# Two PSUM pools throughout instead of a late single ring, and W1-W2 moved behind a cast on GpSimd

## The chip, the cores and the metric

The kernel runs on one core of one Trainium2 chip. The metric is the device time of one execution in microseconds (us). It is compared as a median over several executions. A profiled execution gives, beside its own time, the span from the first to the last instruction and a row for every instruction of each engine: PE (TensorE, with its weight loads as PEld), DVE (VectorE), ACT (ScalarE), POOL (GpSimd) and SP (the queue that issues nearly all DMAs).

## The reference

A cross attention between 512 tokens `x` and 32 state rows in each of 8 batches x 8 heads (64 elements per head) is followed by a feed-forward layer with two input matrices.

```python
scores = scale * x @ state.T;   a  = softmax(scores);   xread = a  @ state
scores2 = scale * state @ x.T;  a2 = softmax(scores2);  sread = a2 @ x
y = concatenate([xread, sread], axis=2)      # per batch 544 tokens of 512 elements
h1 = y @ w1; h2 = y @ w2                     # 512 -> 1024
out = maximum(h1, h2) @ w_out                # 1024 -> 512
```

The maximum is rewritten as `max(h1, h2) = relu(y @ (w1 - w2)) + y @ w2`, so that the layer is `relu(y @ (W1-W2)) @ w_out + y @ (W2 w_out)`. The kernel calls `[W1-W2 | W2 w_out]` Wc: 1024 + 512 columns, three chunks of 512. For the 512 tokens of a batch, `y` is `a @ state`, so the product of the states with Wc (512 rows against 1536 columns, `SW[b]`) is made once per batch, and `a` is multiplied with that.

## The kernel before

All is written out by hand in the order in which it is issued; no scheduler changes it. Each engine runs its own instructions in that order, and so does SP with its DMAs.

**Setup.** SP first loads states and x of batch 0, W2 and W_out in pieces, W1 in two pieces, x of batch 1, the remaining states, x of batch 2. The weights are cast to bf16 on DVE and ACT (`w_cast`), W_out on POOL (`wo_cast`), W2 is transposed and multiplied with W_out (`w_wo`), which gives the third chunk of `wcat`. The first two chunks, W1-W2, are made by POOL in four pieces of 256 columns (`w_sub(0)` to `w_sub(3)`, line 389).

**A batch** goes through these steps. The x tile is cast into `xp` by POOL (`cast_x`, line 72) and once more into the compact `xc` by ACT (`compact_x`), which a DMA transposes into `xt` (`d_xt`). `u_exp` (lines 221, 224) makes the scores of two groups of heads on PE and their exponentials on ACT. `u_norm` makes sums and reciprocals on DVE (lines 228, 230) and multiplies them in on DVE or POOL (`a`, line 231). `u_sr` reads the states' side (line 244), its normalised result `sr` is transposed in `u_srt` (line 268) and copied into `sread_t` by ACT. `a` is transposed by DMA (`d_at`), in batches 0 and 1 by PE (`u_at`, line 262) and copied into `aT` by DVE. `u_sw` makes the chunks of `SW[b]` on PE (line 283, `sw_mm`), with two PSUM banks each, which DVE and ACT copy out into `swt`. `l1` (lines 311, 299, 301) makes eight tiles of relu, alternating between ACT and DVE, and `l2` adds up four output chunks (`l2_open` line 322, `l2_add` line 326, `l2_close`), each in one bank.

**Two terms.** While `wcat` isn't there, `sw_mm` multiplies the states with w1 and the negated states with w2: 16 matmuls in place of 8 for a chunk. Before, this is so for batch 0 and for chunk 1 of batch 1; chunk 0 of batch 1 uses `wcat`.

**PSUM.** There are eight banks. In the setup and for batch 0, four belong to the pool `ps` and four to the pool `acc`, which holds the sums of `w_wo` and of the output chunks. Ahead of the loop over batches 1 to 7, `one_ring` closes both and opens one pool of eight banks, used for everything in turn.

**Around the change** the order is written out so: the steps of batch 0, with `w_sub(0)` and `w_sub(1)` issued on POOL ahead of `l1(0)`; then the second cast of w1, `compact_x(1)`, `d_xt(1)`, `cast_x(1)`, `w_sub(2)`, `w_sub(3)`, the cast of the remaining states (`cast_states("P", rest)`), `load_x(3)`, the DMA transposes of the states (`d_states`, tile `sT`); then the scores of batch 1, its softmax (first half multiplied on DVE, second on POOL) and its `u_sw`, mixed with the closing of batch 0. In the loop, `fillers(b)` puts the steps of batch b+1 between the output chunks of batch b.

Of the kernel before, what the change touches and what calls it, by code (L numbers as in the profile page):

```python
# [15 lines left out]
def kernel(  # L16
# [24 lines left out]
    TWO = 2  # L41
# [6 lines left out]
    keep = ctx.enter_context(tc.tile_pool(name="keep", bufs=2))  # L48
    big = ctx.enter_context(tc.tile_pool(name="big", bufs=2))

    early = ctx.enter_context(ExitStack())
    pools = dict(ps=early.enter_context(tc.tile_pool(name="ps", bufs=4, space=bass.MemoryType.PSUM)),
                 acc=early.enter_context(tc.tile_pool(name="acc", bufs=4, space=bass.MemoryType.PSUM)))
    ctx.enter_context(tc.manual_schedule())

    def bank(dtype=F32, kind="ps"):
        return pools[kind].tile([128, 512 if dtype == F32 else 1024], dtype, tag="b", name=kind)

    def acc():
        return bank(kind="acc")  # L60

    def one_ring():
        early.close()
        pools["ps"] = pools["acc"] = ctx.enter_context(tc.tile_pool(name="ring", bufs=8, space=bass.MemoryType.PSUM))

    def copy(eng, o, i):
        if eng == "A":
            nc.scalar.copy(o, i)  # L68
        elif eng == "V":
            nc.vector.tensor_copy(o, i)  # L70
        else:
            nc.gpsimd.tensor_copy(o, i)  # L72
# [68 lines left out]
    def cast_states(eng, bs):  # L141
        qs = slice(2 * bs.start, 2 * bs.stop)
        copy(eng, s_bf[:, qs], s_f[:, qs].unsqueeze(2).to_broadcast([128, qs.stop - qs.start, 2, D]))
# [36 lines left out]
    def cast_x(b, parts=(("P", slice(0, 8)),)):  # L180
        new_x(b)
        xp = st[b]["xp"] = xio.tile([128, H, NC, 66], BF16, tag="xp", name="xp")
        nc.gpsimd.memset(xp[:, :, :, 64:65], 1.0)
        for e, hs in parts:
            copy(e, xp[:, hs, :, 0:64], xf_t[b][:, hs].rearrange("p h (c d) -> p h c d", c=NC))
# [87 lines left out]
    swt = consts.tile([128, 2, 2, WC], BF16)  # L273

    def sw_mm(b, ch, engs="VA"):
        pg = [bank(), bank()]
        two = b < TWO and ch < 2 and (b, ch) != (1, 0)
        terms = ((sbd, w1b), (sneg, w2b)) if two else ((sbd, wcat),)
        for k, (sv, w) in enumerate(terms):
            for i in range(4):  # L280
                for g in range(2):
                    gs = slice(64 * g, 64 * g + 64)
                    nc.tensor.matmul(pg[g][32 * i:32 * i + 32, :],  # L283
                                     sneg[gs, b, i, :] if k else sbd[gs, b, 2 * i + g, g, :],
                                     w[gs, i, ch * 512:(ch + 1) * 512],
                                     start=(k == 0), stop=(k == len(terms) - 1))
        return lambda: [copy(engs[g], SW[b][:, g, ch * 512:(ch + 1) * 512], pg[g]) for g in range(2)]

    def u_sw(b, *chs):
        for out_of in [sw_mm(b, ch) for ch in chs]:  # L290
            out_of()
# [43 lines left out]
    def l2_out(b):  # L335
        nc.sync.dma_start(out=out[b * L:b * L + S].rearrange("(p c) n -> p c n", c=NC), in_=OB[b][0])
# [50 lines left out]
    def w_sub(q):  # L387
        cs = slice(q * 256, (q + 1) * 256)
        nc.gpsimd.tensor_sub(wcat[:, :, cs], w1f[:, :, cs], w2f[:, :, cs])  # L389

    def w_cast(o, w, ch, engs="VA"):
        cs = slice(ch * 512, (ch + 1) * 512)
        for k in range(2):
            copy(engs[k], o[:, 2 * k:2 * k + 2, cs], w[:, 2 * k:2 * k + 2, cs])
# [77 lines left out]
    for i in range(4):  # L472
        w_wo(2, i)
    w_cast(w1b, w1f, 0)
    w_sub(0)
    w_sub(1)
    for i in range(4):
        w_wo(3, i)
    u_sw(0, 0)
# [6 lines left out]
    compact_x(1, 1)  # L486
    d_xt(1)
    cast_x(1)
    w_sub(2)
    w_sub(3)  # L490
    cast_states("P", rest)
    load_x(3)
    sT = d_states(rest)
# [23 lines left out]
    u_sw(1, 2)  # L517
    u_srt(1)
    l2_out(0)
    one_ring()  # L520
    for b in range(1, B):
        fill = fillers(b)
        if b + 2 < B:
# [39 lines left out]
```

The softmax here doesn't subtract the row's maximum and nothing guards it: scores larger than these inputs give would overflow.

## Time and profile before

| | |
|---|---|
| time, median of 4 runs | 154.5 us (153.93 to 155.42) |
| the profiled execution's own time | 154.03 us |
| its span | 152.1 us, 3012 instructions |
| PE busy | 140.2 us, 92% of the span |
| DVE, ACT, POOL busy | 83.7, 75.3, 43.6 us |
| mean granted TensorE clock | 0.989 |
| HBM read, written | 15.20 MB, 8.91 MB |

Busy time is the time in which an engine had an instruction; its share is a mean over the whole span. The chain that ended last is followed back from the last instruction, at each step to what released it, and shows what set the time at each place. In a timeline each row has start, duration, engine, line, operation, output and inputs, and in brackets how long the engine had been idle before it and what ended that.

### The profile page before, as it was taken

What the parts mean: (1) busy time and instruction counts of PE and PEld (TensorE: products, weight loads), DVE (VectorE), ACT (ScalarE), POOL (GpSimd) and SP (SyncE); (2) the same over time, 40 slices, a digit from 0 to 9 for tenths busy, and PEclk for the clock granted to TensorE, in tenths of its full rate; (3) what the DMA queues carried; (4) which work ended last, traced back from release to release, by engine and by line L of the source; (5) the groups of instructions that cost most, each with busy time, mean ns of one, the idle gap of its engine ahead of it and who ended that gap; (6) DMA issues with size and microseconds to landing.
All of it is one profiled execution on the core that took longest, in us unless ns stands there. A gap on an engine that the chain in (4) does not pass through costs nothing.

```text
span 152.1 us, 3012 instructions
## 1 busy us (share of the span) xinstructions
PE 140.2 (92%) x1236; PEld 68.1 (45%) x1255; DVE 83.7 (55%) x151; ACT 75.3 (50%) x126; POOL 43.6 (29%) x44
## 2 busy tenths in 40 slices
PE   6769999998889999999999999889999999999990
PEld 1357543333445444444454454335434534664460
DVE  5368658527965487545576554645566546631120
ACT  3056259925864656546394636553656226621010
POOL 3025219993830820190046007200500050000000
PEclk9977999999999999999999999999999999999999
DMA  4999999998999498829966992990099022602423
GB/s 92 348 397 387 387 383 328 290 154 253 113 237 286 169 192 299 266 59 209 287 214 114 264 285 101 109 378 0 2 144 343 0 34 41 274 0 67 140 101 113
DMA packets 37934, 29.89 MB, mean 196 GB/s; under 512 B 24864, under 2 KB 33312, under 8 KB 37024
## 3 DMA queue, kind: packets, MB, share of 16 engines
q1 hardware_dynamic: 37776, 29.56, 70.5%
q8 instruction: 10, 0.16, 0.4%
q10 hardware_dynamic: 144, 0.13, 0.3%
q14 instruction: 4, 0.03, 0.1%
HBM read 15.20 MB, written 8.91 MB: 159 GB/s over the span
## 4 chain that ended last, share of the span: by engine, by line
PE 61%; DMA 19%; SPq 8%; ACT 3%; DVE 2%; issue 2%; POOL 2%; ACTq 0%; POOLq 0%
PE acc L326 25%; PE ps L311 16%; DMA xf<-in_x_dram 10%; PE acc L322 6%; DMA aT<-a 6%; SPq L102 4%; SPq L105 3%; DMA xt<-xc 3%; PE ps L370 2%; PE acc L380 2%; PE ps L221 2%; PE ps L283 2%; POOL a L231 2%; PE acc L360 1%; ACT xc L68 1%
## 5 line engine op out<-in xcount | busy, mean ns | idle before, releaser
L326 PE MATMUL acc<-wo,r 128*128 128x512 bf16 x244 | 58.1, 379 | 0.3 <-issue 0.2
L326 PEld LDWEIGHTS <-r 128*128 128x128 bf16 x248 | 23.9, 98 | 28.8 <-issue 0.6
L301 DVE TENSOR_SCALAR r<-ps 128x512 bf16<-128x512 f32 x32 | 22.1, 692 | 17.8 <-PE ps L311 17.7
L231 POOL TENSOR_TENSOR a<-e,er 128x512 bf16<-128x512 bf16 x13 | 13.4, 1050 | 63.0 <-ACT e L224 31.0
L311 PE MATMUL ps<-aT,swt 128*128 128x512 bf16 x122 | 28.8, 379 | 2.5 <-DMA aT<-a 1.3
L70 DVE COPY ob<-acc 128x512 f32<-128x512 f32 (+1 forms) x17 | 11.4, 672 | 27.3 <-PE acc L326 25.5
L299 ACT ACTIVATE r<-ps 128x512 bf16<-128x512 f32 x32 | 19.2, 600 | 9.7 <-PE ps L311 9.2
L311 PEld LDWEIGHTS <-swt 128*128 128x128 bf16 x128 | 12.0, 98 | 16.9 <-issue 1.9
L68 ACT CAST swt<-ps 128x512 bf16<-128x512 f32 x24 | 12.9, 592 | 12.5 <-PE ps L283 12.4
L322 PE MATMUL acc<-swt,aT 128*128 128x512 bf16 x56 | 16.7, 380 | 1.0 <-issue 1.0
L68 ACT COPY ob<-acc 128x512 f32<-128x512 f32 (+1 forms) x16 | 9.2, 576 | 15.9 <-PE acc L326 10.9
L70 DVE CAST swt<-ps 128x512 bf16<-128x512 f32 x24 | 15.3, 682 | 1.8 <-PE ps L283 1.7
L224 ACT ACTIVATE e<-ps 128x512 bf16<-128x512 f32 x16 | 8.8, 595 | 14.7 <-PE ps L221 14.7
L72 POOL CAST xp<-xf 128x2048 bf16<-128x2048 f32 (+1 forms) x8 | 14.1, 1765 | 6.4 <-DMA xf<-in_x_dram 6.4
L68 ACT CAST xc<-xf 128x1024 bf16<-128x1024 f32 x14 | 13.9, 1050 | 0.2 <-DMA xf<-in_x_dram 0.2
L228 DVE TENSOR_REDUCE es<-e 128x16 f32<-128x512 bf16 x16 | 10.6, 662 | 2.3 <-ACT e L224 2.3
L389 POOL TENSOR_TENSOR wcat<-w1f,w2f 128x1024 bf16<-128x1024 f32 x4 | 9.8, 2476 | 3.1 <-DMA w1f<-in_moe_w_dram 3.1
L136 PE MATMUL ps<-warm 128*128 128x512 bf16 x14 | 6.1, 579 | 1.5 <-POOL warm L122 1.3
L322 PEld LDWEIGHTS <-aT 128*128 128x128 bf16 x62 | 4.7, 98 | 5.9 <-issue 2.6
L415 PE MATMUL acc<-wo,w2t 128*128 128x512 bf16 x31 | 7.2, 379 | 0.1
L283 PE MATMUL ps<-wcat,sbd 64*32 64x512 bf16 x168 | 6.7, 380 | 0.1
L221 PE MATMUL ps<-sbd,xt 128*128 128x64 bf16 x128 | 5.6, 199 | 1.1 <-DMA xt<-xc 0.6
(68 smaller groups left out, 103.8 us busy)
## 6 DMA issues: line engine op xcount, KB each, us to landing
xf<-in_x_dram SPq DMA_DIRECT2D x8, 1024.0 KB, 8.8
out_dram<-ob SPq DMA_DIRECT2D x7, 1024.0 KB, 5.0
w2f<-in_moe_w_dram SPq DMA_DIRECT2D x2, 1024.0 KB, 10.5
wof<-in_moe_w_out_dram SPq DMA_DIRECT2D x4, 512.0 KB, 11.3
w1f<-in_moe_w_dram SPq DMA_DIRECT2D x2, 1024.0 KB, 14.8
out_dram<-ob SPq DMA_DIRECT2D x3, 256.0 KB, 2.8
out_dram<-obs SPq DMA_DIRECT2D x8, 64.0 KB, 1.7
s_f<-in_state_dram SPq DMA_DIRECT2D x1, 320.0 KB, 13.7
```

Source lines behind the costliest of these rows:

```text
L68: nc.scalar.copy(o, i)
L70: nc.vector.tensor_copy(o, i)
L72: nc.gpsimd.tensor_copy(o, i)
L228: nc.vector.tensor_reduce(d["es"][:, g], d["e"][:, g].rearrange("p i c n -> p (i c) n"), axis=mybir.AxisListType.X, op=ALU.add)
L231: mul.tensor_mul(d["a"][:, g].rearrange("p c i n -> p i c n"), d["e"][:, g], d["er"][:, g].rearrange("p (i c) -> p i c", i=4).unsqueeze(3) ...
L283: nc.tensor.matmul(pg[g][32 * i:32 * i + 32, :], sneg[gs, b, i, :] if k else sbd[gs, b, 2 * i + g, g, :], w[gs, i, ch * 512:(ch + 1) * 512 ...
L299: nc.scalar.activation(out=o, in_=p, func=ACTF.Relu)
L301: nc.vector.tensor_scalar(o, p, scalar1=0.0, scalar2=None, op0=ALU.max)
L311: nc.tensor.matmul(p, SW[b][:, g, f * 128:(f + 1) * 128], AT[b][:, g, :], start=(g == 0), stop=(g == 1))
L322: nc.tensor.matmul(OB[b][1 + c], AT[b][:, g, c * 128:(c + 1) * 128], SW[b][:, g, FF:WC], start=(g == 0), stop=False)
L326: nc.tensor.matmul(OB[b][1 + c], R[b][:, f, c * 128:(c + 1) * 128], wo[:, f, :], start=False, stop=(f == NF - 1))
L389: nc.gpsimd.tensor_sub(wcat[:, :, cs], w1f[:, :, cs], w2f[:, :, cs])
```

## The change

The pools `ps` and `acc` stay as they are for the whole kernel: `one_ring` and its call are gone. So that `u_sw` still finds its six banks at once, the two banks of the third Wc chunk come from `acc` for batches from 2 on. Chunk 0 of batch 1 is made in two terms as chunk 1 is, which adds eight matmuls. `w_sub(0)` and `w_sub(1)` are issued behind `cast_x(1)`, together with the other two. On SP, DVE and ACT the order of instructions stays the same; only the bank that some copies read has another name.

```diff
-    early = ctx.enter_context(ExitStack())
-    pools = dict(ps=early.enter_context(tc.tile_pool(name="ps", bufs=4, space=bass.MemoryType.PSUM)),
-                 acc=early.enter_context(tc.tile_pool(name="acc", bufs=4, space=bass.MemoryType.PSUM)))
+    pools = {k: ctx.enter_context(tc.tile_pool(name=k, bufs=4, space=bass.MemoryType.PSUM)) for k in ("ps", "acc")}
...
-    def one_ring():
-        early.close()
-        pools["ps"] = pools["acc"] = ctx.enter_context(tc.tile_pool(name="ring", bufs=8, space=bass.MemoryType.PSUM))
...
     def sw_mm(b, ch, engs="VA"):
-        pg = [bank(), bank()]
-        two = b < TWO and ch < 2 and (b, ch) != (1, 0)
+
+        pg = [bank(kind="acc" if ch == 2 and b > 1 else "ps") for g in range(2)]
+        two = b < TWO and ch < 2
...
     w_cast(w1b, w1f, 0)
-    w_sub(0)
-    w_sub(1)
     for i in range(4):
         w_wo(3, i)
...
     cast_x(1)
-    w_sub(2)
-    w_sub(3)
+    for q in range(4):
+        w_sub(q)
     cast_states("P", rest)
...
     l2_out(0)
-    one_ring()
     for b in range(1, B):
```

## The prediction

> **What bounds the kernel now.** I read the totals first, then the chain that ended last in order of time, then the timelines of POOL, DVE and PE around the places that the diff touches, and last the groups of single lines for durations.
>
> ```profile
> PE 140.2 (92%) x1236; PEld 68.1 (45%) x1255; DVE 83.7 (55%) x151; ACT 75.3 (50%) x126; POOL 43.6 (29%) x44
> PE 61%; DMA 19%; SPq 8%; ACT 3%; DVE 2%; issue 2%; POOL 2%; ACTq 0%; POOLq 0%
> ```
>
> TensorE sets the pace and POOL looks idle. That is an average. From 42 us on, the chain is matmuls of one batch after the other, 13.96 us each (l1 starts at 42.35, then at 56.31). Before that it is a chain of hand-overs, and the change lies there:
>
> ```profile
> 12.81 15.01 DMA xf<-in_x_dram
> ...
> 27.84 1.99 ACT xc L68 x2
> 29.83 0.03 ACT swt L68
> 29.86 4.80 DMA xt<-xc
> ...
> 36.78 0.69 DVE a L231
> ...
> 39.55 0.61 PE ps L262 x8
> ...
> 42.13 0.18 ACT sread_t L68
> 42.31 0.04 issue
> 42.35 3.62 PE ps L311 x16
> ```
>
> x(1) lands at 27.82, is compacted, transposed, and goes through the scores of batch 1 to the eight transposes of `u_at(1)` (L262) at 39.55 and to `l1(1)` (L311) at 42.35. PE's own row there reads "[0.83 <-ACT sread_t L68]": it was free 0.83 us before. POOL in that stretch:
>
> ```profile
> 22.14 5.16 POOL L389 TENSOR_TENSOR wcat<-w1f,w2f 128x1024 bf16<-128x1024 f32 x2 [3.05 <-DMA w1f<-in_moe_w_dram]
> 27.25 0.24 POOL L183 MEMSET xp<- 128x32 bf16 x1
> 27.87 1.91 POOL L72 CAST xp<-xf 128x2048 bf16<-128x2048 f32 x1 [0.38 <-DMA xf<-in_x_dram]
> 29.75 4.67 POOL L389 TENSOR_TENSOR wcat<-w1f,w2f 128x1024 bf16<-128x1024 f32 x2
> 34.34 1.26 POOL L72 CAST s_bf<-s_f 128x1280 bf16<-128x1280 f32 x1
> 38.50 1.05 POOL L231 TENSOR_TENSOR a<-e,er 128x512 bf16<-128x512 bf16 x1 [2.90 <-PE ps L244]
> ```
>
> The reader is to see three things: two subtractions fill the wait for x(1); POOL has 2.90 us to spare before its half of a(1); and that half ends at 39.55, the very time at which PE starts `u_at(1)`.
>
> **The subtractions move.** In the new order POOL waits for x(1) with nothing to do, casts it at 27.87 to 29.78, and then has all four subtractions ahead. Rows follow each other at 2.30 us here (29.75, 32.05, 34.34), so the third starts at 34.34, the fourth at 36.64, the cast of the remaining states at 38.94 and ends at 40.20, and a(1)'s second half can run 40.23 to 41.28. That is 1.73 us after 39.55, with nothing else disturbed. PE has no other work to put there: it is in order, and behind `u_at(1)` stand the last adds of batch 0, `u_sw(1,2)`, the transpose of sr and `l1(1)`. From the transposes on, the way to `l1(1)` is: 0.22 (the second four; the first four need DVE's half alone) + 0.96 (39.99 to 40.95) + 0.34 (40.95 to 41.29) + 0.06 = 1.58 us. Then its second tile needs the bank that ACT empties after ob and swt (41.05 to 42.13 before, 1.08 us), which holds it about 0.4 us. So `l1(1)` runs as if it had begun at T + 1.98, with T the start of the second four transposes: 41.3 + 1.98 = 43.3, or +0.95 us against 42.35.
>
> **What it meets on DVE.** The third and fourth subtraction now run while DVE does the softmax of batch 1. They meet one DVE instruction that reads two SBUF tensors as the subtraction does: the product a (L231), at 36.78, 0.14 us after the fourth has started. The trace of before doesn't show this pair, but it shows neighbours:
>
> ```profile
> L389 POOL TENSOR_TENSOR wcat<-w1f,w2f x4: 2346/2353/2853, 22.1 to 32.1; 128x1024 bf16<-128x1024 f32 x4
> L70 DVE CAST w1b<-w1f x2: 694/774/853, 22.1 to 27.2; 128x1024 bf16<-128x1024 f32 x2
> L231 DVE TENSOR_TENSOR a<-e,er x3: 691/693/744, 12.9 to 36.8; 128x512 bf16<-128x512 bf16 x3
> ```
>
> The 2853 ns subtraction is the first, at 22.14, which began while DVE's cast of w1b ran (22.09 to 22.78): it lost 0.50 us of an overlap of 0.64. The 853 ns cast began at 27.18 inside a subtraction that ended at 27.31, and a POOL memset followed until 27.49: it lost 0.16. The 744 ns product began at 12.88 inside a POOL cast that ended at 13.08: it lost 0.05 of 0.20. Each late comer ends as if it had waited for the other, less 0.14.
>
> Lower bound: a loses 0.05, as its own row did; then +0.95 stands. Upper bound: the 853 ns cast outlasted the memset behind the subtraction too, so a may wait out the states' cast as well, until 40.20. Value taken, by the 2853 ns row (longest overlap): a waits until the fourth subtraction ends, 36.64 + 2.36 = 39.00, and takes 0.55 more. It ends at 39.55, not 37.47. Everything behind it on DVE moves by that: es and er (which POOL's half of a needs), ob of chunk 0, two swt, rr, sr, ob of chunk 2, and the copy aT, without which `l1(1)` can't begin. DVE had no gap from 37.39 to the end of aT at 41.69:
>
> ```profile
> 41.01 0.68 DVE L70 COPY aT<-ps 128x1024 bf16<-128x1024 bf16 x1
> ```
>
> So aT ends near 43.85 and `l1(1)` starts at 43.9: **+1.55 us**. POOL's side agrees: the states' cast, now behind a, ends at 40.75, a(1) at 41.8, T = 41.85, and T + 1.98 = 43.83. With the upper bound aT ends at 45.0 and the shift is +2.7.
>
> [...]
>
> **The pools.** The single ring goes, and with it the wait at 42.35, which ended with ACT's sread_t at 42.29. In the new kernel the first tile of `l1(1)` takes the bank that aT empties (41.69 before), so 0.6 us of the 0.83 would be free. It is already counted: 43.9 holds no such wait, with it the start would be some 0.6 later. With four banks the fifth tile of l1 needs the first relu. In a later batch ACT does ob, sread_t and that relu from 56.46 to 57.70, and the fifth tile starts 4 x 0.43 after 56.31, at 58.04: 0.34 us to spare. `l1(0)` already ran on four banks, 8 matmuls in 1.89 us (32.22), as fast as 16 in 3.62. Cost 0. If that cover went, ACT being late by one more copy (0.59), it is 0.25 us a batch. The third Wc chunk in the adding banks takes those of chunks 3 and 0, emptied microseconds before; its copies on ACT and DVE keep their order. Cost 0.
>
> **Eight more matmuls** in `u_sw(1,0)`: by the two forms of L283, a two-term chunk holds PE 0.56 us (37.44 to 38.00), a wcat chunk 0.35 (36.13 to 36.48), so 0.2 us. PE now waits for T anyway, which hides it; without that wait it is 0.2 on the path. Its wait for POOL's wcat goes, which had been met.
>
> **SP's queue.** The transposes of the states (issued at 35.63) wait for the states' cast, so until 40.2 to 40.75. Queued behind them on SP: xt(2) (40.67), the output of batch 0 (43.77), x(4) (44.38). With 2.22 us for the states' issue, xt(2) is issued at 43.0 and lands 4.3 to 5.3 later, by 48.3; `u_exp(2)` needs it at 47.97 + 1.55 = 49.5. x(4) is 2 us later, and its cast is not due before POOL's next product, 8 us on. The DMA engines then are busy to about 53.2 rather than 51.2, and the next aT transfer (52.23, now 53.8) comes just after. If it were caught, its landing would go from 3.3 to the 5.1 us that one of the six took, less 0.8 spare: 1.0 us. I count 0 and keep it for the range. In the stretch from 22 to 27 DVE's casts become free of POOL (0.16 us); x(1)'s landing hides that.
>
> **Sum.** Span 152.1 + 1.55 = 153.65; with the 1.9 us around the span, 154.03 becomes 155.6. The profiled run is 0.47 below the median of the four, 154.5, so against the median the forecast is **156.1 us** (+1.0%).
>
> **Rivals.** (1) POOL and DVE hardly hinder each other: +0.95, 155.5 us. For it: the 0.05 us of the 744 ns row; against: 0.50 lost at 22.14. (2) POOL goes from instruction to instruction without letting DVE in, a waits until 40.20: +2.7, 157.2 us. For it: the 853 ns cast; against: at 8 us POOL's cast of xp (0.865 us) got in between two DVE casts. (3) The other side: POOL's second half of a is there before it decides. If T falls below 42.35 - 1.98 = 40.37, the freed ring wait shows and `l1(1)` starts up to 0.6 earlier: 153.9. It needs POOL 0.95 us quicker than its rows say over six instructions; nothing speaks for that but that spans on POOL are rough. (4) Four banks are too few in every batch: 6 x 0.25 on top, 157.6 us; against it the 0.34 us to spare.
>
> **How the numbers follow.** Forecast 0.45, rival 1 0.17, rival 2 0.27, rival 3 0.05, rival 4 0.06. The four runs spread by 1.5 us, so each case has some 0.5 us to both sides. The range 154.7 to 157.8 leaves out most of rival 3 and the tails. About 1% (1.5 us) is what a measurement of this kernel can tell from no change, so 156.05 parts same from slower, through the middle of the forecast: slower 0.56 (half the forecast, nearly all of 2 and 4), same 0.41 (the other half, rival 1, rival 3), faster 0.03.
>
> **What would show it.** Right: POOL's cast of xp(1) near 27.9, four L389 rows (in the new file their number differs) back to back, the states' cast ending at 40.2 to 40.8, DVE's product a near 2.8 us long or late in its end, L311's first row near 43.9 and no idle time put down to sread_t; batches 13.96 us apart. Rival 1: a stays at 0.7 us and L311 starts at 43.3. Rival 2: a ends after 40.5 and L311 starts near 45. Rival 4: idle time on L311 put down to ACT or DVE in every batch. It is wrong altogether if L311 starts before 42.4.

## The result, and the profile after

| | before | changed |
|---|---|---|
| time, median over all executions | 155.04 us (152.17 to 158.15, 16) | 154.63 us (153.67 to 155.32, 11) |
| ratio changed / before | | 1.0103, 95% interval 1.0053 to 1.0152 |
| profiled execution: time, span | 154.03, 152.1 us | 154.06, 152.2 us |
| its `l1(1)` starts | 42.35 us | 44.01 us |
| its `l1(1)` to `l1(7)` | 85.37 us | 83.76 us |

The ratio compares, of each kernel, only executions near its fastest. So there are two results: by the ratio the change costs 1.0%, about 1.6 us, while the medians over all executions come out nearly equal. The experiments below show why: in both traced executions of before some batches wait for a transpose that comes late, and in the changed kernel's trace none does. The two profiled executions have the same time, and that is where the trace must be read most carefully: a loss of 1.66 us and a gain of 1.61 us meet in it. Line numbers of the changed kernel are five or six lower: its L225, L306 and L384 are L231, L311 and L389 of the kernel before.

The totals and the chain's shares of the changed kernel, and the clock row, each digit 3.8 us:

```profile
PE 139.8 (92%) x1244; PEld 69.1 (45%) x1263; DVE 87.2 (57%) x151; ACT 75.3 (49%) x126; POOL 44.0 (29%) x44
PEclk9955999999999999999999999999999999999999
PE 82%; DVE 8%; DMA 4%; issue 2%; ACT 1%; SPq 0%
```

DVE has 3.5 us more busy time with the same 151 instructions, and 8% of the chain instead of 2%. The timelines of POOL and DVE (start, duration, engine) show which instructions grew:

```profile
27.61 1.89 POOL L66 CAST xp<-xf 128x2048 bf16<-128x2048 f32 x1 [8.72 <-DMA xf<-in_x_dram]
29.46 9.73 POOL L384 TENSOR_TENSOR wcat<-w1f,w2f 128x1024 bf16<-128x1024 f32 x4
39.14 1.71 POOL L66 CAST s_bf<-s_f 128x1280 bf16<-128x1280 f32 x1
40.82 1.04 POOL L225 TENSOR_TENSOR a<-e,er 128x512 bf16<-128x512 bf16 x1
```

```profile
27.82 2.23 DVE L64 CAST w1b<-w1f 128x1024 bf16<-128x1024 f32 x1
37.06 2.69 DVE L225 TENSOR_TENSOR a<-e,er 128x512 bf16<-128x512 bf16 x1
43.28 0.68 DVE L64 COPY aT<-ps 128x1024 bf16<-128x1024 bf16 x1
```

POOL waits 8.72 us for x(1), casts it, and makes all four pieces of W1-W2 until 29.46 + 9.73 = 39.19. DVE's product a starts at 37.06 inside the fourth, takes 2.69 us instead of 0.69, and ends at 39.75. What stands behind it is the stretch of the chain that ended last:

```profile
37.06 2.69 DVE a L225
39.74 0.61 DVE es L222
40.35 0.02 issue
40.37 0.25 DVE er L224
40.62 0.55 DVE ob L64
41.17 1.19 DVE swt L64 x2
42.36 0.09 DVE rr L242
42.45 0.02 issue
42.47 0.29 DVE sr L243
42.76 0.60 DVE ob L64
43.36 0.61 DVE aT L64
43.97 0.04 issue
44.01 3.62 PE ps L306 x16
```

DVE runs from a to aT without a gap, and `l1(1)` begins when aT is there. The rows of `l1` in PE's timeline, first changed, then before, tell the rest:

```profile
44.01 3.62 PE L306 MATMUL ps<-aT,swt 128*128 128x512 bf16 x16 [0.23 <-DVE aT L64]
57.97 3.62 PE L306 MATMUL ps<-aT,swt 128*128 128x512 bf16 x15
```

```profile
84.23 3.62 PE L311 MATMUL ps<-aT,swt 128*128 128x512 bf16 x15
99.47 3.61 PE L311 MATMUL ps<-aT,swt 128*128 128x512 bf16 x15 [1.11 <-DMA aT<-a]
113.76 3.61 PE L311 MATMUL ps<-aT,swt 128*128 128x512 bf16 x15 [0.17 <-DMA aT<-a]
```

In the changed kernel every later batch takes 13.96 us. In before's execution the fifth `l1` came after 15.24 and the sixth after 14.29 us, both after a wait for the DMA transpose aT: 1.28 + 0.33 = 1.61 us that the changed kernel doesn't have. 1.66 - 1.61 is the whole difference. That loss was in before's profile all along; the prediction saw a landing of aT in "the 5.1 us that one of the six took" and asked only whether the change would cause one more.

### The profile page after: what moved, and what is told of

Same layout as the page of the kernel before. It is cut to its first block, busy times and chain, and to the rows that moved or that the text cites. A ratio compares the mean times of both kernels' runs of the same rounds, so it can differ in the third digit from the quotient of the medians.

```text
span 152.2 us, 3021 instructions
## 1 busy us (share of the span) xinstructions
PE 139.8 (92%) x1244; PEld 69.1 (45%) x1263; DVE 87.2 (57%) x151; ACT 75.3 (49%) x126; POOL 44.0 (29%) x44
## 4 chain that ended last, share of the span: by engine, by line
PE 82%; DVE 8%; DMA 4%; issue 2%; ACT 1%; SPq 0%
PE acc L321 32%; PE ps L306 18%; PE acc L317 8%; PE acc L410 5%; DMA xf<-in_x_dram 4%; PE ps L278 3%; PE ps L215 3%; PE ps L365 2%; PE acc L375 2%; PE ps L238 2%; DVE a L225 2%; PE ps L399 2%; PE acc L355 1%; DVE w1b L64 1%; PE ps L197 1%
## 5 line engine op out<-in xcount | busy, mean ns | idle before, releaser
L225 POOL TENSOR_TENSOR a<-e,er 128x512 bf16<-128x512 bf16 x13 | 13.4, 1049 | 58.6 <-ACT e L218 30.0
L306 PE MATMUL ps<-aT,swt 128*128 128x512 bf16 x122 | 28.8, 379 | 0.8 <-DVE aT L64 0.2
L306 PEld LDWEIGHTS <-swt 128*128 128x128 bf16 x128 | 12.2, 98 | 14.8 <-DVE swt L64 0.5
L62 ACT CAST swt<-ps 128x512 bf16<-128x512 f32 x18 | 10.0, 588 | 13.8 <-PE ps L278 13.7
L64 DVE CAST swt<-ps 128x512 bf16<-128x512 f32 x18 | 11.6, 681 | 0.7 <-PE ps L278 0.7
L384 POOL TENSOR_TENSOR wcat<-w1f,w2f 128x1024 bf16<-128x1024 f32 x4 | 9.7, 2458 | 0.0
L130 PE MATMUL ps<-warm 128*128 128x512 bf16 x14 | 5.3, 510 | 1.6 <-POOL warm L116 1.3
L215 PEld LDWEIGHTS <-xt 128*128 128x128 bf16 x128 | 5.1, 101 | 2.6 <-ACT xt L62 0.7
```

The source lines that it names most:

```text
L215: nc.tensor.matmul(p[:, k * 64:k * 64 + 64], d["xt"][:, 4 * i + 2 * g + cp, :], sbd[:, b, 2 * i + g].rearrange("p u n -> p (u n)"), start= ...
L225: mul.tensor_mul(d["a"][:, g].rearrange("p c i n -> p i c n"), d["e"][:, g], d["er"][:, g].rearrange("p (i c) -> p i c", i=4).unsqueeze(3) ...
L306: nc.tensor.matmul(p, SW[b][:, g, f * 128:(f + 1) * 128], AT[b][:, g, :], start=(g == 0), stop=(g == 1))
```

## The experiments

The question was first whether DVE's product a really waits for the subtraction, then why the late transposes come and go. Theory A: moving the subtractions costs 1.5 to 2 us at `l1(1)`, pools and two terms nothing. Rivals: the four banks cost something in every batch (B); later, the place of DMAs on SP's queue decides the late transposes (C), or the length of PE's instruction stream does (D).

**The pools alone**: the changed kernel with the subtractions put back and chunk 0 of batch 1 from `wcat`.

```diff
-        two = b < TWO and ch < 2
+        two = b < TWO and ch < 2 and (b, ch) != (1, 0)
...
     w_cast(w1b, w1f, 0)
+    w_sub(0)
+    w_sub(1)
...
-    for q in range(4):
-        w_sub(q)
+    w_sub(2)
+    w_sub(3)
```

> The two pools of four banks throughout, as in the changed kernel, but the four subtractions where they were and chunk 0 of batch 1 from wcat. Theory (the loss comes from the moved subtractions alone; the pools free the wait at the start of l1(1)): DVE's first product a takes 0.69 us, u_at(1) starts at 39.5 to 39.6, l1(1) at about 41.75 in place of 42.35, batches stay 13.96 us apart; 0.6 us less than before, ratio 0.996. Rival (four banks are too few, the pools cost something in every batch): idle time on PE at the first tiles of l1 in each batch, ratio 1.00 to 1.01.

Measured: 156.66 us, ratio 1.0217 (1.0147 to 1.0287). It missed. In the profiled execution, at 159.48 us the longest of the six, the product a took 0.69 us, as expected, yet each of the next five batches took 14.7 to 15.0 us. (`l1(1)` itself came at 44.64 in it, as `l1(0)` had not begun before 27.24.) That looks like rival B, but PE's rows name another releaser than a bank's copy:

```profile
59.36 3.61 PE L306 MATMUL ps<-aT,swt 128*128 128x512 bf16 x16 [0.60 <-DMA aT<-a]
74.39 1.89 PE L306 MATMUL ps<-aT,swt 128*128 128x512 bf16 x8 [0.91 <-DMA aT<-a]
```

**The subtractions alone**: before, with `w_sub(0)` and `w_sub(1)` moved behind `cast_x(1)`, ring and `wcat` kept.

```diff
     w_cast(w1b, w1f, 0)
-    w_sub(0)
-    w_sub(1)
...
-    w_sub(2)
-    w_sub(3)
+    for q in range(4):
+        w_sub(q)
```

> The kernel before with its single ring and with wcat for chunk 0 of batch 1; only the first two subtractions are moved behind the cast of x(1). Theory (the moved subtractions hold DVE's product a until the fourth has ended): a takes about 2.7 us, u_at(1) starts near 41.85, the ring's wait for sread_t is back, so l1(1) starts near 44.5, 2.1 to 2.2 us later than before; ratio 1.014. Rival (the pools or the eight matmuls cause the loss): a at 0.69 us, l1(1) at 42.35, ratio 1.000.

Measured: 159.67 us median of 6 (155.52 to 160.85). The product a took 2.53 us, as A has it; the four subtractions end at 38.67, a at 39.22:

```profile
29.40 9.27 POOL L389 TENSOR_TENSOR wcat<-w1f,w2f 128x1024 bf16<-128x1024 f32 x4
36.69 2.53 DVE L231 TENSOR_TENSOR a<-e,er 128x512 bf16<-128x512 bf16 x1
```

`l1(1)` came at 45.47 instead of the 44.5 expected: four matmuls ahead of it took 1.91 us instead of 1.03, at a granted clock of 0.50 from 42 to 44 us. Four later batches came late as well: three after a wait for aT, the first by the trace after ACT's ob, with aT landing 0.13 us ahead of it. So the time tells the two apart badly; the row of a is what this run is good for.

**The last subtraction behind a(1)**: the changed kernel with `w_sub(3)`, the states' cast and their transposes after POOL's half of a.

```diff
-    for q in range(4):
+    for q in range(3):
         w_sub(q)
-    cast_states("P", rest)
     load_x(3)
-    sT = d_states(rest)
...
     u_sc(1, 1, nc.gpsimd)
+    cast_states("P", rest)
+    sT = d_states(rest)
+    w_sub(3)
```

> The changed kernel with the fourth subtraction and the cast of the remaining states (with its DMA transposes) moved behind POOL's half of a(1), so that POOL has nothing to do when DVE's product a comes. Theory (a waits for the subtraction that runs): a takes 0.69 us, u_at(1) starts at 39.6 to 39.9, l1(1) at 41.8 to 42.1, 0.3 to 0.6 us less than before, ratio 0.996 to 0.998. Rival (the first three subtractions behind the cast of x(1), or the eight matmuls, already cost what the change costs): ratio 1.005 to 1.010.

Measured: 151.82 us (151.55 to 152.67, 12 executions), ratio 0.9919 (0.9885 to 0.9953): faster than both kernels. Its timelines of POOL, DVE and PE:

```profile
29.85 6.97 POOL L384 TENSOR_TENSOR wcat<-w1f,w2f 128x1024 bf16<-128x1024 f32 x3
38.39 1.05 POOL L225 TENSOR_TENSOR a<-e,er 128x512 bf16<-128x512 bf16 x1 [1.58 <-DVE er L224]
```

```profile
36.46 0.91 DVE L225 TENSOR_TENSOR a<-e,er 128x512 bf16<-128x512 bf16 x1
```

```profile
41.63 3.62 PE L306 MATMUL ps<-aT,swt 128*128 128x512 bf16 x16 [0.22 <-DVE aT L64]
```

Even here a met the end of the third subtraction (36.82) and ended 0.55 us after it. With a nearly free, `l1(1)` starts at 41.63, 0.72 before that of the kernel before: the wait for the ring's bank is gone (its row names aT, not sread_t), and only the late a hid it in the changed kernel.

**The kernel before, once more**, as a control.

> The kernel before, unchanged, once more in a profile. If the two late landings of aT in batches 5 and 6 (PE idle 1.1 and 0.3 us there) belong to the kernel, they are here again at the same batches; if they belong to that execution, they are gone and all batches are 13.96 us apart, with a span 1.4 to 1.5 us shorter. l1(1) starts at 42.35 +- 0.3 in either case.

Measured: 155.18 us. `l1(1)` at 42.39; the `l1` of batches 4 and 5 waited 1.03 and 1.12 us for aT, batch 6 0.19. So neither outcome exactly: the late transposes are there again, in one batch more.

To find what makes aT late, the DMA view of before was narrowed to the four microseconds of one late transpose (95.4 to 99.4; a digit is 0.1 us and the busy share of the 16 DMA engines in tenths):

```profile
DMA  4999999999998799999999980000000000008999
DMA packets 2009, 0.52 MB, mean 131 GB/s; under 512 B 2008, under 2 KB 2008, under 8 KB 2008
q1 hardware_dynamic: 2008, 0.51, 125.2%
q8 instruction: 1, 0.02, 1.4%
aT<-a SPq DMA_TRANSPOSE x1, 5.1
```

From 97.8 to 99.0 the row reads 0. 24 of the transposes' 256 B packets, 0.02 us each otherwise, take 1.3 to 1.4 us here (1.1 to 1.6 over all late batches traced); they start from 97.59 on and the last ends at 99.06. Just ahead of them stands the single packet of q8, 16 KB of instructions, from 97.29 to 98.21. The page counts ten such packets in an execution (`q8 instruction: 10, 0.16, 0.4%` in before). The trace of before has 1255 weight loads of PE, 129 between two `l1`, and 12 other instructions beside the matmuls; with one matmul to each load (1236 have a row) these are 2522 instructions, and some 258 in a batch; ten packets for 2522 are one for some 250, about one batch of PE. That q8 feeds PE is inferred from this. The read therefore comes at nearly the same place of each batch. Set against the issue of aT on SP (times from the trace's DMA packets), with the distance from one `l1` to the next:

| kernel | PE instr. | read starts after aT's issue, us, batches 2 to 6 | batch, us |
|---|---|---|---|
| before | 2522 | 5.2, 5.3, 5.3, 3.1, 0.9 | 13.96, 13.96, 13.96, 15.24, 14.29 |
| before, control | 2522 | 5.2, 5.3, 3.0, 3.1, 0.9 | 13.97, 13.96, 15.15, 15.24, 14.32 |
| subtractions alone | 2522 | 2.6, 2.9, 3.0, 3.1, 0.9 | 14.70, 15.09, 15.13, 15.23, 13.96 |
| pools alone | 2516 | 2.8, 3.0, 3.0, 3.1, 2.9 | 14.72, 15.03, 15.04, 14.95, 14.95 |
| changed | 2532 | 0.5, 0.5, 0.1, -0.3, -0.3 | 13.96 in all |
| last subtraction late | 2532 | 1.0, 0.4, -0.1, -0.2, 0.2 | 13.96, 14.25, 13.97, 13.96, 13.96 |

A read that starts 2.6 to 3.1 us after aT's issue falls among the transposes' packets (the first comes 1.2 us after the issue) and costs the batch 0.7 to 1.3 us, in all 12 batches above. At 1.0 us or less it costs at most 0.36, at 5.2 or more nothing. (The 14.25 is no late aT: two copies on DVE, at 55.10, met POOL's cast of x, at 54.53, took 2.17 us, against 0.98 in before, where POOL was idle, and held up the relu of `l1`.) This speaks for D, and the next three kernels were made to test it.

**Pools and two terms, subtractions early**: the changed kernel's PE instructions, and before's order on POOL.

```diff
     w_cast(w1b, w1f, 0)
+    w_sub(0)
+    w_sub(1)
...
-    for q in range(4):
-        w_sub(q)
+    w_sub(2)
+    w_sub(3)
```

> The changed kernel with its pools and its eight extra matmuls, but with the first two subtractions back ahead of l1(0). Its PE instructions are those of the changed kernel, one for one. Theory (of the whole: the moved subtractions cost about 1.6 us at l1(1); where the 16 KB reads of PE's instructions fall decides whether aT lands late, and the eight matmuls moved them to a harmless place): a takes 0.69 us, l1(1) starts at 41.5 to 41.9, every batch is 13.96 us apart, 2 us or more less than the changed kernel, ratio to the kernel before 0.985 to 0.992. Rival (the two pools of four banks cost something in every batch, as the slow run with the pools alone might say): batches of 14.5 to 15 us again, ratio 1.01 to 1.02.

Measured: 151.35 us (151.11 to 152.96), ratio 0.9923 (0.9813 to 1.0032). The product a took 0.69 us and all batches take 13.96 us. Between this kernel and the pools alone, 156.66 us, stand only the eight matmuls of `u_sw(1,0)`, which *lengthen* the work: 5.3 us less, or 2.9% by the ratios. Rival B falls here, since the pools are the same in both. (`l1(1)` came at 42.99 in the profiled execution, not at 41.5 to 41.9; in it `l1(0)` was already 1.8 us later than in the kernel with the last subtraction late.)

**Before, with eight small matmuls more** in the first warm-up, far ahead of everything disputed. They write an unused result.

```diff
-    def warm_up(n):
+    def warm_up(n, small=0):
...
+        for k in range(small):
+            nc.tensor.matmul(p[:, 0:64], warm[:, 0:128], warm[:, 0:64], start=(k == 0), stop=(k == small - 1))
...
-    warm_up(6)
+    warm_up(6, 8)
```

> The kernel before with eight small matmuls (64 columns, on zeros, result unused) more in the first warm-up, at 4 us, where PE has time; nothing else. Theory (the place of the instruction reads against the aT transposes decides): with 16 PE instructions more each batch's read comes earlier, before or at the first packet of aT; aT lands in 3.0 to 4.0 us in every batch, all batches are 13.96 us apart, l1(1) is still at 42.35; fastest runs like the fastest of before (152), but the slow ones of 155 to 158 are gone; median 152 to 153, ratio of fast runs 0.985 to 0.995. Rival (late landings are chance, or come from x loads and outputs): aT lands late in one to three batches as before, ratio 1.00.

Measured: 152.14 us (151.56 to 152.37), against 156.2 of before measured beside it (151.81 to 157.27, 11 executions), so 4.1 us less for more work; the ratio, taken as above, is 0.9952 (0.9869 to 1.0035) and can't tell the two apart. `l1(1)` starts at 42.33 and all batches take 13.96 us; the reads start -0.3 to 0.4 us after aT's issue. The first and last `l1` of its batches 1 to 7, and the same four microseconds as above:

```profile
42.33 3.62 PE L313 MATMUL ps<-aT,swt 128*128 128x512 bf16 x16 [0.83 <-ACT sread_t L68]
126.09 3.62 PE L313 MATMUL ps<-aT,swt 128*128 128x512 bf16 x15
```

```profile
DMA  6999999999997579999999999999999999999972
DMA packets 3121, 0.78 MB, mean 196 GB/s; under 512 B 3121, under 2 KB 3121, under 8 KB 3121
q1 hardware_dynamic: 3121, 0.78, 105.5%
aT<-a SPq DMA_TRANSPOSE x1, 3.3
```

No q8 packet, no hole, 0.26 MB more moved, and aT lands in 3.3 instead of 5.1 us. Order on POOL, DVE and SP and the pools are those of before, so C falls.

**The changed kernel without its eight matmuls**: chunk 0 of batch 1 from `wcat`.

```diff
-        two = b < TWO and ch < 2
+        two = b < TWO and ch < 2 and (b, ch) != (1, 0)
```

> The changed kernel with chunk 0 of batch 1 from wcat, so without the eight extra matmuls; pools and moved subtractions stay. Theory (instruction reads): PE's instructions are again as many as in the run with the pools alone, the reads fall 2 to 3 us after aT is issued, aT lands in 4.8 to 5.1 us in three to five of the batches 2 to 6 and each of them takes 15 us; l1(1) near 44.0 as in the changed kernel; 158 to 160 us, ratio 1.03 to 1.04. Rival (the eight matmuls are only work that the wait for POOL hides): same time as the changed kernel, 154 to 155, ratio 1.01.

Measured: 158.68 us (157.79 to 160.25), ratio 1.0383 (1.0256 to 1.0509), as expected. The reads start 2.6 to 3.1 us after aT's issue, and PE's rows show both effects side by side:

```profile
43.96 3.62 PE L306 MATMUL ps<-aT,swt 128*128 128x512 bf16 x16 [0.22 <-DVE aT L64]
58.63 3.61 PE L306 MATMUL ps<-aT,swt 128*128 128x512 bf16 x15 [0.53 <-DMA aT<-a]
73.29 3.61 PE L306 MATMUL ps<-aT,swt 128*128 128x512 bf16 x15 [0.54 <-DMA aT<-a]
88.15 3.61 PE L306 MATMUL ps<-aT,swt 128*128 128x512 bf16 x15 [0.74 <-DMA aT<-a]
103.29 3.61 PE L306 MATMUL ps<-aT,swt 128*128 128x512 bf16 x15 [1.02 <-DMA aT<-a]
118.26 3.61 PE L306 MATMUL ps<-aT,swt 128*128 128x512 bf16 x15 [0.85 <-DMA aT<-a]
```

`l1(1)` is where the changed kernel has it (44.01), so the eight matmuls are worth nothing there; then 58.63 to 118.26 are four batches of 14.9 us in the mean instead of 13.96. This run also speaks against the clock as the cause: PE's mean granted clock was 0.997 here and five batches were late, while the changed kernel's was 0.53 from 8 to 12 us and 0.62 from 12 to 16 (the two 5 in its row), 1.00 from 20 us on, and it had none.

**More of the subtractions late**: as with the last one, and also `w_sub(2)`, both halves of a(1) on POOL, the states put in two fillers earlier.

```diff
-    for q in range(4):
+    for q in range(2):
         w_sub(q)
...
-    u_sc(1, 0, nc.vector)
+    u_sc(1, 0, nc.gpsimd)
     u_sc(1, 1, nc.gpsimd)
+    cast_states("P", rest)
+    sT = d_states(rest)
+    w_sub(2)
+    w_sub(3)
...
-            fill[11].append(lambda: put_states(rest, sT))
+            fill[9].append(lambda: put_states(rest, sT))
```

> A version meant to beat both kernels: the kernel with the fourth subtraction late, and besides the third one late too, both halves of a(1) multiplied on POOL, which is then free, and the copy of the states' transposes into sbd put one output chunk earlier, where DVE has time. Theory (DVE's gapless row from es to aT sets the start of l1(1)): DVE is rid of 0.7 to 0.9 us there, l1(1) starts at 40.7 to 41.0 in place of 41.63, batch 1 takes 13.96 in place of 14.25; about 150.7 us, ratio 0.985. Rival (POOL's 1.05 us for the product or u_at's place on PE sets it): l1(1) at 41.6 or later, ratio 0.992.

Measured: 151.92 us, ratio 0.9939 (0.9861 to 1.0017). A miss: by the median no better than the last subtraction alone. (The start of `l1(1)` can't be compared to the tenth: x(1) was cast at 28.59 in this execution, at 27.99 in the other.) DVE is relieved, but the second tile of `l1(1)` now waits for ACT's copies:

```profile
41.66 0.59 PE L306 MATMUL ps<-aT,swt 128*128 128x512 bf16 x2
42.49 3.18 PE L306 MATMUL ps<-aT,swt 128*128 128x512 bf16 x14 [0.23 <-ACT swt L62]
```

## Why the prediction was right, and what it had wrong

**The main term held.** +1.55 us at `l1(1)` was forecast, +1.66 measured; 43.9 against 44.01. The steps were those of the text: a ends 0.55 us after the fourth subtraction (forecast 39.55, measured 39.75), es, er, ob, two swt, rr, sr, ob and aT follow without a gap, POOL's half of a starts at 40.82 and ends at 41.86 (forecast 41.8). The pure comparison is with the kernel before plus eight small matmuls, which has no late transpose either: `l1(1)` at 42.33 against 44.01, 1.68, and profiled times of 152.29 against 154.06, 1.77. In the prediction's working the end of aT is 0.08 us too high (41.69 + 2.08 is 43.77, not 43.85), which changes nothing.

**The fit of the total is in part luck.** The forecast of 1.0% fits the ratio of 1.0103, but the executions of before in that ratio aren't free of late batches: the profiled one, with its 1.61 us, is among them. Against the kernel with eight small matmuls more, 152.14 us, the changed kernel's median is 2.5 us longer, or 1.6%, of which the late a explains 1.7. And as a time the forecast missed: 156.1 us, built on before's executions with their late batches, lies 1.5 us above the median of 154.63, which falls just below the stated range of 154.7 to 157.8.

**Rivals 1 and 2 fall by the same number.** Where a began inside a subtraction, its end stands 0.55 us behind the end of that subtraction in four kernels: 39.19 to 39.75 in the changed one, 38.67 to 39.22 with the subtractions alone, 39.15 to 39.70 without the eight, 36.82 to 37.37 with the last one late. So it is no mild slowdown (rival 1), and POOL doesn't go on to the states' cast first (rival 2): that cast takes 1.71 us instead of 1.26, which is a's 0.55 less an overlap. In the changed kernel a took 2.69 us, against 0.69 us where no subtraction ran (before).

**Rival 3's mechanism was real, its condition wasn't met.** The freed bank gives `l1(1)` 0.72 us when a is in time (41.63 with the last subtraction late). **Rival 4 fell**: 13.96 us a batch on four banks, and the third chunk in the adding banks cost nothing.

**SP's queue** went as forecast: the states' transposes at 40.88, xt(2) at 42.31 (forecast 43.0), x(4) at 46.01, all hidden.

**The term that was mis-sized: "Eight more matmuls".** The text had them cost 0.2 us, hidden. They are hidden, but the instructions count in another way: they move the 16 KB reads off the transposes (2.6 to 3.1 us after aT's issue without them, 0.5 us or less with them). Without them the changed kernel takes 158.68 instead of 154.63 us, 4.0 us more. Next to it the landing of aT ("I count 0 and keep it for the range", up to 1.0 us) had the wrong sign and cause: before already paid 1.61 us in the profiled execution, and the changed kernel doesn't. The step that failed was to treat the one landing of 5.1 us, shown in before's profile, as a meeting of data transfers, without looking at what was on the DMA engines in it.

**Not foreseen:** DVE's cast of w1b began at 27.82, 0.21 us after POOL's cast of x(1), and took 2.23 us instead of 0.85. In this execution PE's granted clock was 0.53 from 8 to 12 us and 0.62 from 12 to 16 (0.73 and 0.84 in before's), and `l1(0)` started at 25.27 instead of 24.65. It cost nothing at `l1(1)`: without the eight matmuls the cast took 0.69 us and `l1(1)` was at 43.96.

**What stays open.** Which instruction of PE lets a read begin isn't known: the place moves by more than the count alone would give, and in the same kernel the read of batch 4 falls at 5.3 in one execution and 3.0 in the other. Nor is it shown why some of the transposes' packets stand still, from 0.3 us after the read's start until 0.85 us after its end (97.59 to 99.06 in before); that they do so in all 17 late batches traced is. The subtractions' price by medians, 154.63 against 151.35 us, is 3.3; the late a (1.66) and the freed bank that it hides (0.72) make 2.4 of it, the rest wasn't traced. Of before only two executions were traced, so that its longer ones, up to 158.15 us, are long for the same reason is likely but not shown.

## What to carry to other kernels

In the four kernels here in which DVE's product a began inside a GpSimd subtraction (2.3 to 2.4 us each), it ended 0.55 us after that subtraction and took up to 2.93 us instead of 0.69, so long GpSimd work belongs behind the short one that DVE needs next, not ahead of it; here three lines moved make the difference of 154.63 to 151.82 us. When one transfer of several lands late, look at what else was on the DMA engines in those microseconds before it is called chance. And where a small edit makes many later batches longer or shorter, count PE's instructions: with eight idle matmuls more, early in the kernel before, the median was 152.14 us against 156.2, and no batch of the traced execution was late.

## What the runs showed of the hardware

The 16 KB reads of q8 (ten in an execution of before; that they are PE's instructions is inferred) weren't free beside DMA transposes here. Where one started 2.6 to 3.1 us after aT's issue, some 20 packets of 256 B (24 in before's) took 1.1 to 1.6 us, aT landed after 4.6 to 5.1 instead of some 3.3 us, and the batch took 14.7 to 15.2 instead of 13.96 us. Where it started at most 1.0 us after the issue, or 5.2 us and more, the batch took at most 14.32 us.
